# A longer hand-written order of first steps, and 22 idle one-column products, in a one-core mLSTM and mixture-of-experts kernel

## The chip, the cores and the metric

The kernel runs on one core of a Trainium2 chip. The metric is the device time of one execution, in microseconds (us). The kernel before was timed three times: 759.41, 755.95 and 760.29 us, median 759.41. One more execution was profiled; all rows below are from it.

Engines: PE multiplies matrices (TensorE), PEld is its loading of weights, DVE is VectorE, ACT ScalarE, POOL GpSimd, and SP issues most DMAs.

## What is computed

```python
for t in range(S):                              # mLSTM: 4 batches, 8 heads, 768 tokens, 40 wide
    m_new = np.maximum(f_gate[:, :, t] + m, i_gate[:, :, t])
    f_stab = np.exp(f_gate[:, :, t] + m - m_new)
    i_stab = np.exp(i_gate[:, :, t] - m_new)
    C = f_stab * C + i_stab * outer(vt, kt)
    n = f_stab * n + i_stab * kt
    y[:, :, t] = sigmoid(o_gate[:, :, t]) * (C @ qt) / np.maximum(np.abs(n @ qt), 1.0)
x = y as 3072 x 320
x = np.maximum(x @ w_in, 0) ** 2 @ w_out        # dense layer, 2048 wide
idx = argmax(x @ w_gate)                        # one of 8 experts for each token
out = gate_w * (np.maximum(x @ w1[idx], 0) @ w2[idx])
```

## The kernel before

**Attention.** The recurrence is computed in 24 chunks (4 batches of 6) of 128 tokens. A chunk's parts have short names: `kv`, `qk`, `de` load its values, keys with queries, and decays; `ca`, `cb` (method `causal`, L673 and L674, POOL) add a bias to the decays' two halves and mask them, `ea`, `eb` (`decay`, L680, ACT) take exp of them; `ra`, `rb` (`round`, L642 on ACT and L645 four times on POOL) split the two operands of the scores; `sc` are the scores (L778, PE), `wa`, `wb` their weighing (DVE), `va`, `vb` the product with the values (L791), `up` and `in` the state's update and use (L717), `di`, `ga` the division and gate (DVE), `tu` the turning into columns (L725, L727, PE). The rounded operands `kq` have one buffer: a chunk's rounding can start only when the scores of the chunk before it have read it. Only chunks from number 7 on (`WHOLE = 7`) are rounded.

**Dense layer.** Tokens stand in 8 groups of 384 (three chunks each). Step (g, f) is for group g and the f-th 128 of the layer's 2048 hidden values: `l` is the first layer (8 products, L863, result `hp`), `m` the second (9 products, L896 to L898, added up in three `acc`). Between the two stand `sa` (ACT: L871 and L872 make `gh`) and `sb` (DVE: L880 and L883 make `gl`; `sbP` does it on POOL). The weights are decoded once, one f after the other, in the steps `A` (load), `R`, `T`, `S`, `W`, `H`, `L`, on ACT, DVE and POOL. The first two groups are walked together in halves (`SHARED = 2`, `PART = 8`), so 32 steps belong to them.

**Gate.** When a group's last step is done, `fin(g)` adds the residual rows on DVE (L979), turns the rows on PE (L952, result `lpt`), copies them on ACT (L956, result `scr`), takes logits (L961), picks the expert on DVE and counts ranks on PE (L1031, L944, result `pr`). It is a generator that advances by one `next` for each later step of the dense layer.

**Order.** The kernel is scheduled by hand: what the program writes first, an engine runs first. `PLAN` is a list of words, each of which writes the part of its name (function `token`): `sc6` the scores of chunk 6, `l12` the first layer of step 12, `f7` seven idle products of 512 columns. After the list a loop takes over: for each further step it writes `attend()` and `layer1()`, then `attend()` and `layer2()`. `attend()` adds QUICK (5/4, as long as 32 or fewer `l` have been written) or STEP (9/16, after that) to a count, and writes half a chunk for each whole number in it. In the last group of the loop, 38 (`ACT_APART`) ACT instructions on a one-element tile `void` are spread in between.

**Routed experts.** Behind the dense layer the program has 15 unrolled units of each of two widths on PE (`unit_narrow0` to `14`, `unit_wide0` to `14`); after each it jumps or falls through to the next unit, narrow or wide by the token count. In this input the order is narrow 0, wide 1, 2, 3, narrow 4 to 7, wide 8, 9, narrow 10. A unit's first-layer products have line L295, its second-layer ones L314 to L316.

Of the kernel before, what the change touches and what calls it, by code (L numbers as in the profile page):

```python
# [53 lines left out]
XC_DVE = 2  # L54
FETCH = 3
PERIOD = 6
ACT_APART = 38
STILL, AFTER = 3, 18
APART = 59

# [2 lines left out]
WHOLE = 7  # L63
KVO = 3
QK0, QK1, ROUND0, ROUND1 = 1, 3, (3, 4), (1, 2)
SHARED, PART, QUICK = 2, 8, 5 / 4
PLAN = """
    g0 A0 g1 g2 R0 kv0 g3 qk0 g4 TQ0 g5 A1 f7 g6 de0 ea0 f3 g7 g8 g9 qk1 S0 W0 sc0 vw0 eb0 g10 A2 H0 g11 R1 wa0 kv1 wb0 de1 T1 S1 th0 ea1 va0 vb0 eb1 R2
    up0 T2 vw1 W1 LV0 sc1 H1 SA2 g12 di0 ga0 tu0 de2 ca2 um0 qk2 cb2 wa1 A3 wb1 up1 kv2 um1 f3 va1 ou0 vb1 de3 sc2 ea2 th1 eb2 g13 L1 R3 di1 th2 vw2 wa2
    f3 va2 wb2 f4 vb2 ga1 qk3 ca3 di2 A4 f2 up2 g14 ga2 tu1 tu2 um2 cb3 W2 ou2 sc3 in3 TP3 ou1 S3 ea3 H2 eb3 wb3 L2 l0 R4 wa3 sa0 kv3 W3 TQ4 sbP0 vw3 l1  # L70
    sd3 de4 S4 H3 l2 W4 th3 sa1 A5 va3 sb1 sa2 cb4 L3 vb3 H4 ca4 up3 R5 qk4 sb2 um3 T5 m0 di3 SA5 kv4 m1 de5 sc4 m2 ea4 ga3 vw4 cc3 L4 A6 wa4 l3 W5 in4
    up4 eb4 wb4 th4 sa3 cb5 l4 sb3 qk5 A7 um4 tu3 H5 R6 TP6 va4 cc4 sa4 sd4 LV5 m3 vb4 kv5 ou3 l5 sc5 ca5 in5 A8 di4 qk6 SA6 de6 W6 ea5 ga4 sbP4 wa5 A9 m4
    eb5 R7 wb5 H6 TP7 va5 sd5 SA7 sa5 vw5 L6 vb5 W7 l6 de7 A10 di5 tu4 th5 sbP5 up5 ga5 m5 H7 R8 sa6 sb6 tu5 ou4 L7 ou5 R9 l7 TP8 um5 m6 TP9 cc5 l8 SA8
    sa7 W8 sb7 S9 kv6 H8 LV8 W9 cb6 l9 R10 sa8 sa9 l10 sb8 A11 m7 l11 in6 sa10 ca6 A12 H9 ea6 TP10 sb9 l12 vw6 sb10 m8 sc6 LV9 R11 S10 sd6 R12 W10 m9 sa11
    sb11 TP11 cb7 m10 eb6 A13 sa12 l13 l14 S11 W11 sbP12 m11 z H10 m12 sa13 sb13 T12 R13 l15 wb6 sa14 wa6 T13 eb7 S12 LV10 W12 S13 sa15 l16 sb14 A14 R14
    A15 up6 H11 l17 LV11 m13 T14 W13 H12 sa16 qk7 sbP15 R15 m14 sbP16 S14 m15 um6 sa17 LV12 l18 m16 W14 cc6 l19 ca7 sa18 l20 va6 sb17 T15 H13 th6 S15 sa19
    LV13 H14 m17 sb18 vb6 ea7 l21 W15 H15 m18 L14 ra7 sa20 sb19 sa21 l22 LV15 sb20 di6 sb21 m19 sa22 l23 m20 m21 ga6 sbP22 rb7 m22 sa23 sb23 m23 tu6 l24
    ou6 kv7 sa24 l25 sb24 sa25 sb25
""".split()


W1, WN = 3072, 5632
# [298 lines left out]
def kernel(ctx, tc, qk, q3, kvo, gates, w_io, wg, w12, cst, out, dbg=None):  # L381
    nc = tc.nc
# [20 lines left out]
    apart = front.tile([128, 512], F32, name="apart")  # L403
# [304 lines left out]
    def ahead(m, name, *a):  # L708
        if (m, name, *a) not in over:
            over.add((m, name, *a))  # L710
            assert name != "decay" or m < ON_PE or (m, "causal", *a) in over
            getattr(chunks[m], "decays_early" if name == "decays" and m < ON_PE else name)(*a)
# [195 lines left out]
    ones = const.tile([128, 128], BF16, name="ones")  # L908
# [221 lines left out]
    def turn(x, *a):  # L1130
        if count[x] < len(turns[x]):
            fn, i = turns[x][count[x]]
            count[x] += 1
            fn(i, *a)
# [53 lines left out]
    with tc.manual_schedule():  # L1188
# [30 lines left out]
        def layer1():  # L1219
            q = l1(*its[nl[0]])  # L1220
            gs[nl[0]] = next(q)
            late.append(q)
            late_of[nl[0]] = [q, 0]
            nl[0] += 1

        def layer2():
            i = nd[0]
            g, f = its[i]
            if f == 0 or (g < SHARED and f == PART):
                accs[g] = accumulators()  # L1230

            if g == NG - 1 and f >= NF - 3:
                l2(g, accs[g], range(2), f, *gs[i])
            else:
                l2(g, accs[g], range(3), f, *gs[i])
                gs.pop(i)
            nd[0] += 1
            if g < SHARED and f == PART - 1:
                for t, acc in enumerate(accs.pop(g)):
                    nc.scalar.activation(out=(xrl if g % 2 else xr2)[:, t, 64:384], in_=acc[:, 0:DM], func=ACTF.Copy)  # L1240
            if (g, f) == (FETCH, 0):
                x = nc.sync.value_load(e0, min_val=0, max_val=E - 1)
                nc.sync.dma_start(out=raw.rearrange("p (o n) -> p o n", o=1), in_=w12[bass.ds(x, 1)].rearrange("o p n -> p o n"))
            if f == NF - 1:
                if g == NG - 1:
                    for j in range(i - 2, i + 1):
                        l2(g, accs[g], [2], its[j][1], *gs.pop(j))
                q = fin(g, accs.pop(g))
                next(q)
                before = list(fins)  # L1250
                fins.append(q)
                if g == NG - 2:
                    leave(brief)
                    p0 = ctx.enter_context(tc.tile_pool(name="p0", bufs=1, side="right"))
                    w0.extend([p0.tile([128, WN], F32R, name="w0h"), p0.tile([128, W1], F32R, name="w01l")])
                    fins.append(first_unit(before, p0))
                if g == NG - 1:
                    leave(dense)
                    fins[:] = [last_tokens(q)]
# [134 lines left out]
        def token(word):  # L1394
            k = len(word.rstrip("0123456789"))
            name, i = word[:k], int(word[k:] or 0)
            if name in turn_of:
                x, *a = turn_of[name]
                assert count[x] == i, (word, count[x])
                turn(x, *a)  # L1400
            elif name in names:
                what = names[name]
                ahead(i, *((what[:-1], int(what[-1])) if what[-1].isdigit() else (what,)))
            elif name == "sc":
                mains[i].run("scores0")
                mains[i].run("scores1")
            elif name in parts:
                mains[i].run(parts[name])
            elif name == "g":
                next(gt)  # L1410
            elif name == "f":
                for _ in range(i):
                    nc.tensor.matmul(apart, ones, ones.rearrange("p (o n) -> p o n", o=1).to_broadcast([128, 4, 128]), start=True, stop=True)
            elif name == "l":
                assert nl[0] == i
                layer1()
            elif name in ("sa", "sb", "sbP"):
                if name == "sbP":
                    on_pool.add(its[i])
                late_of[i][1] += 1  # L1420
                assert late_of[i][1] == (1 if name == "sa" else 2)
                next(late_of[i][0])
                if name != "sa":
                    late.remove(late_of[i][0])
            elif name == "m":
                assert nd[0] == i
                layer2()
            else:
                {"z": constants}[name]()
# [3 lines left out]
        for word in PLAN:  # L1433
            token(word)
        late.sort(key=lambda q: [i for i in late_of if late_of[i][0] is q])
        catch_up()
        while nd[0] < len(its):
            i = nd[0]
# [6 lines left out]
            while nl[0] < min(i + 1 + AHEAD, len(its)):  # L1445
                g1, f1 = its[nl[0]]
# [19 lines left out]
            if g == NG - 1:  # L1466
                for k in range(ACT_APART * f // NF, ACT_APART * (f + 1) // NF):
                    nc.scalar.activation(out=void, in_=void, func=ACTF.Copy)
# [31 lines left out]
    m2, idx, tab, xs, gts = [rest_of[n] for n in "m2 idx tab xs gts".split()]  # L1500
# [78 lines left out]
```

## Time and profile before

| | |
|---|---|
| three runs | 759.41, 755.95, 760.29 us |
| the profiled execution's own time | 755.73 us |
| its span in the trace | 753.9 us |
| PE busy | 731.4 us (97%) |
| DVE, ACT, POOL busy | 493.0, 418.7, 357.1 us |
| mean granted PE clock | 0.993 |

The span is the part of the execution that the trace shows; 1.8 us of the execution's time lie around it. In a profile row, "idle before <-X" is the time that the engine stood still ahead of the instruction, and X is what ended the wait; `<-issue` means that nothing in the trace ended it. [...] "x4" counts instructions that were put together in a row.

### The profile page before, as it was taken

Reading aid. Unit: us, or ns where it says so; the run is one execution under the profiler, and the core shown is the slowest. Engines: PE = TensorE matmul, PEld = TensorE weight load, DVE = VectorE, ACT = ScalarE, POOL = GpSimd, SP = SyncE. Lnnn points to the kernel's source line nnn. Section 1 sums busy time; section 2 is a strip of 40 time slices with the busy share of each in tenths; the row PEclk is TensorE's granted clock in tenths of the full one; section 3 lists DMA queues with packets and bytes.
Section 4 is the critical chain, followed back from the end, with each engine's and each line's share of the span. In section 5 each row is a group of like instructions: output and inputs, shape, how many; then the busy total and the mean of one; then the engine's idle time right before and its main releaser. Section 6 shows DMA issues by size and latency. Waiting matters only on the chain.

```text
span 753.9 us, 14422 instructions
## 1 busy us (share of the span) xinstructions
PE 731.4 (97%) x5178; PEld 717.9 (95%) x5179; DVE 493.0 (65%) x1140; ACT 418.7 (56%) x809; POOL 357.1 (47%) x419
## 2 busy tenths in 40 slices
PE   9999999798999999999999999999999999999995
PEld 6899999788999999999999999999889999999995
DVE  8798895477666575655675564455466757877563
ACT  5588774444456455455445534663465556776453
POOL 3699355665355355365455401530345325666431
PEclk9999999999999999999999999999999999999998
DMA  7898444554447444364354000100296556877610
GB/s 238 247 286 272 128 122 133 142 154 122 144 133 273 117 131 117 81 181 119 92 152 120 30 33 1 33 33 33 82 352 206 161 168 210 258 227 240 182 45 15
DMA packets 54646, 109.52 MB, mean 145 GB/s; under 512 B 5438, under 2 KB 34283, under 8 KB 54436
## 3 DMA queue, kind: packets, MB, share of 16 engines
q1 hardware_dynamic: 49956, 96.37, 43.6%
q0 software_dynamic: 4128, 11.77, 5.0%
q8 instruction: 48, 0.79, 0.4%
q10 hardware_dynamic: 480, 0.31, 0.2%
q14 instruction: 34, 0.28, 0.1%
HBM read 99.20 MB, written 10.86 MB: 146 GB/s over the span
## 4 chain that ended last, share of the span: by engine, by line
PE 88%; DVE 4%; issue 3%; POOL 2%; DMA 2%; ACT 1%; SPq 0%; POOLq 0%; DVEq 0%
PE hp L863 23%; PE hp L295 13%; PE acc L896 8%; PE acc L898 8%; PE acc L897 7%; PE pv L791 5%; PE op L314 4%; PE op L316 4%; PE op L315 4%; PE sp L778 3%; PE tp L717 3%; PE lp L961 2%; PE xp L281 1%; PE lpt L952 1%; POOL kq L645 1%
## 5 line engine op out<-in xcount | busy, mean ns | idle before, releaser
L645 POOL TENSOR_TENSOR kq<-st,kq 120x256 fp32r<-120x256 f32 x136 | 95.8, 736 | 134.1 <-ACT kq L642 134.1
L896 PE MATMUL acc<-w_h,gh 128*128 128x320 f32 x384 | 125.2, 326 | 0.0
L898 PE MATMUL acc<-w_h,gl 128*128 128x320 f32 x384 | 119.4, 311 | 0.0
L897 PE MATMUL acc<-w_l,gh 128*128 128x320 f32 x384 | 119.0, 310 | 0.0
L880 DVE SCALAR_TENSOR_TENSOR hp<-hp,g 128x384 f32<-128x384 f32 x121 | 67.8, 560 | 74.4 <-ACT g L871 74.3
L871 ACT ACTIVATE g<-hp 128x384 f32<-128x384 f32 x128 | 62.5, 488 | 91.8 <-PE hp L863 90.2
L863 PE MATMUL hp<-xh,w_h 128*128 128x384 f32 x384 | 112.4, 347 | 0.0
L863 PE MATMUL hp<-xh,w_l 128*128 128x384 f32 x384 | 87.3, 335 | 0.0
L264 DVE SCALAR_TENSOR_TENSOR gl<-hp,gh 128x384 fp32r<-128x384 f32 x88 | 47.8, 556 | 60.1 <-ACT gh L234 59.8
L863 PE MATMUL hp<-xl,w_h 128*128 128x384 f32 x256 | 86.9, 339 | 0.0
L883 DVE TENSOR_TENSOR gl<-hp,gh 128x384 fp32r<-128x384 f32 x121 | 67.5, 558 | 14.3 <-ACT gh L872 0.7
L896 PEld LDWEIGHTS acc<-w_h,gh 128*128 128x128 f32 x384 | 73.2, 191 | 0.0
L897 PEld LDWEIGHTS acc<-w_l,gh 128*128 128x128 f32 x384 | 73.1, 190 | 0.0
L898 PEld LDWEIGHTS acc<-w_h,gl 128*128 128x128 f32 x384 | 72.8, 189 | 0.0
L872 ACT ACTIVATE gh<-g 128x384 fp32r<-128x384 f32 x128 | 67.2, 525 | 6.8 <-PE acc L897 2.8
L863 PEld LDWEIGHTS hp<-xh,w_l 128*128 128x128 f32 x384 | 68.9, 188 | 0.0
L863 PEld LDWEIGHTS hp<-xh,w_h 128*128 128x128 f32 x384 | 65.8, 189 | 0.1
L234 ACT ACTIVATE gh<-hp 128x384 fp32r<-128x384 f32 x88 | 43.2, 491 | 40.7 <-PE hp L295 40.2
L642 ACT ACTIVATE kq<-st,cs 120x1024 fp32r<-120x1024 f32 x34 | 39.0, 1147 | 35.2 <-PE sp L778 35.2
L680 ACT ACTIVATE Ab<-Ab 128x512 f32<-128x512 f32 x44 | 27.6, 632 | 54.5 <-POOL Ab L674 54.5
L177 POOL DMA_INDIRECT out_dram<-ot,idx x34 | 41.5, 1222 | 25.5 <-ACT ot L213 18.3
L791 PEld LDWEIGHTS pv<-kvo,Ab 128*128 128x128 f32 x384 | 48.2, 191 | 1.0 <-issue 0.5
(296 smaller groups left out, 1824.0 us busy)
## 6 DMA issues: line engine op xcount, KB each, us to landing
st<-in_qk_dram SPq DMA_DIRECT2D x34, 480.0 KB
raw<-in_w_dram SPq DMA_DIRECT2D x30, 512.0 KB, 4.5
kvo<-in_kvo_dram SPq DMA_DIRECT2D x24, 529.0 KB
raw<-in_w_io_dram SPq DMA_DIRECT2D x16, 704.0 KB
Ab<-A_d SPq DMA_DIRECT2D x44, 256.0 KB
raw<-in_w_dram SPq DMA_DIRECT2D x20, 427.0 KB, 3.7
raw<-in_w_dram SPq DMA_DIRECT2D x10, 426.0 KB, 4.7
q<-in_q_dram SPq DMA_DIRECT2D x20, 180.0 KB
```

The lines of the kernel that those rows point to most:

```text
L264: e.scalar_tensor_tensor(out=gl[:, j], in0=hp[j % 4], scalar=0.0, in1=gh[:, j].bitcast(F32), op0=ALU.max, op1=ALU.subtract).then_inc(sGL, 1)
L295: m = e.matmul(hp[f % 4][:, 0:w], a, c, start=(n == 0), stop=(n == 7))
L645: nc.gpsimd.tensor_tensor(out=o[:, c], in0=self.st[j][:, c], in1=o[:, c].bitcast(F32), op=ALU.subtract)
L791: nc.tensor.matmul(self.pv[:, hd], d.Ab[r][:, i], d.v[:, hd], start=True, stop=True)
L863: nc.tensor.matmul(hp, a, x, start=(n == 0), stop=(n == 7))
L871: nc.scalar.activation(out=r, in_=hp, func=ACTF.Relu)
L872: nc.scalar.activation(out=gh, in_=r, func=ACTF.Square)
L880: e.scalar_tensor_tensor(out=sq, in0=hp, scalar=0.0, in1=r, op0=ALU.max, op1=ALU.mult)
L883: e.tensor_tensor(out=gl, in0=sq, in1=gh.bitcast(F32), op=ALU.subtract)
L896: nc.tensor.matmul(acc[t][:, 0:DM], gh[:, sl], wh, start=begin, stop=False)
L897: nc.tensor.matmul(acc[t][:, 0:DM], gh[:, sl], wl, start=False, stop=False)
L898: nc.tensor.matmul(acc[t][:, 0:DM], gl[:, sl], wh, start=False, stop=end)
```

## The change

`PLAN` gets longer and is put in another order. Before, its words end with `l25` and `m23`, and of chunk 7 it has no more than loads, rounding, mask and exp. Now it ends with the same `l25` and `m23`, but has all of chunk 7 (`sc7` to `ou7`) and of chunk 8 the loads, `ca8`, `cb8`, `ea8`, `eb8` and the rounding `ra8`, `rb8`. `f` words still give 22 products of 512 columns. A new word `e` writes idle products of one column; `e12` and `e10` give 22 of them, each with its load of weights. `QUICK` goes from 5/4 to 3/4, `ACT_APART` from 38 to 29. `sbP` stands 7 times in both lists.

```diff
-ACT_APART = 38
+ACT_APART = 29
...
-SHARED, PART, QUICK = 2, 8, 5 / 4
+SHARED, PART, QUICK = 2, 8, 3 / 4
 PLAN = """
-    g0 A0 g1 g2 R0 kv0 g3 qk0 g4 TQ0 g5 A1 f7 g6 de0 ea0 f3 g7 g8 g9 qk1 S0 W0 sc0 vw0 eb0 g10 A2 H0 g11 R1 wa0 kv1 wb0 de1 T1 S1 th0 ea1 va0 vb0 eb1 R2
...
+    g0 A0 g1 g2 qk0 g3 kv0 g4 R0 g5 TQ0 f7 g6 de0 e12 g7 A1 sc0 A2 qk1 ea0 kv1 g8 vw0 eb0 R1 up0 g9 g10 R2 de2 th0 de1 TP1 g11 S0 W0 wb0 wa0 TQ2 H0 va0
...
+    sa21 l22 sbP20 LV15 m20 l23 ga7 tu6 ra8 tu7 sa22 sb21 sbP22 sa23 l24 kv8 ou6 m21 rb8 sb23 l25 ou7 m22 sa24 sa25 sb24 m23 sb25
 """.split()
...
+            elif name == "e":
+                for _ in range(i):
+                    nc.tensor.matmul(apart[:, 0:1], ones, ones[:, 0:1], start=True, stop=True)
```

**ACT at the end of the words and behind them.** First the order before: the first two rows with L642 are the rounding of chunk 8, and L680 is exp on its two halves, where L956 are the copies of `fin(0)`.

```order
150 L642 ACTIVATE kq<-st,cs 120x1024
151 L871 ACTIVATE g<-hp 128x384
152 L872 ACTIVATE gh<-g 128x384
153 L956 ACTIVATE scr<-lpt 128x384
154 L801 ACTIVATE kvo<-kvo 128x320
155 L642 ACTIVATE kq<-st,cs 120x1024
156 L680 ACTIVATE Ab<-Ab 128x512 x2
157 L871 ACTIVATE g<-hp 128x384
158 L872 ACTIVATE gh<-g 128x384
159 L956 ACTIVATE scr<-lpt 128x384
160 L871 ACTIVATE g<-hp 128x384
161 L872 ACTIVATE gh<-g 128x384
```

Now the order of the changed kernel around the copies of `fin(0)`, where L642 and L680 are those of chunk 9:

```order
159 L956 ACTIVATE scr<-lpt 128x384
160 L642 ACTIVATE kq<-st,cs 120x1024
161 L801 ACTIVATE kvo<-kvo 128x320
162 L642 ACTIVATE kq<-st,cs 120x1024
163 L871 ACTIVATE g<-hp 128x384
164 L872 ACTIVATE gh<-g 128x384
165 L956 ACTIVATE scr<-lpt 128x384
166 L680 ACTIVATE Ab<-Ab 128x512
167 L871 ACTIVATE g<-hp 128x384
168 L872 ACTIVATE gh<-g 128x384
169 L956 ACTIVATE scr<-lpt 128x384
170 L680 ACTIVATE Ab<-Ab 128x512
```

Before, both exps of the next chunk stand ahead of the second copy; now one stands between the second and the third copy, and one behind the third. They belong to chunk 9 now: chunk 8's rounding and exps stand further up, inside the list of words.

**PE at `fin(1)`.** The order before: the products of chunk 10 (`tp`, `sp`) stand ahead of the rank counts `pr` (L1031, L944).

```order
719 L863 MATMUL hp<-xh,w_h 128x384
720 L863 MATMUL hp<-xl,w_h 128x384
721 L863 MATMUL hp<-xh,w_l 128x384 x3
722 L717 MATMUL tp<-C,q_1836 128x126 x3
723 L778 MATMUL sp<-kq 128x128 x4
724 L1031 LDWEIGHTS tri
725 L1031 MATMUL pr<-oh,tri 128x24
```

The changed kernel at the same place: `pr` comes right after the first layer's products.

```order
766 L863 MATMUL hp<-xh,w_h 128x384
767 L863 MATMUL hp<-xl,w_h 128x384
768 L863 MATMUL hp<-xh,w_l 128x384 x3
769 L1031 LDWEIGHTS tri
770 L1031 MATMUL pr<-oh,tri 128x24
```

Behind the last of the counts, the changed kernel goes on like this:

```order
781 L952 MATMUL lpt<-cs,xrl 128x128 x3
782 L896 MATMUL acc<-w_h,gh 128x320
783 L897 MATMUL acc<-w_l,gh 128x320
784 L898 MATMUL acc<-w_h,gl 128x320
785 L896 MATMUL acc<-w_h,gh 128x320
786 L897 MATMUL acc<-w_l,gh 128x320
787 L898 MATMUL acc<-w_h,gl 128x320
788 L896 MATMUL acc<-w_h,gh 128x320
789 L897 MATMUL acc<-w_l,gh 128x320
790 L898 MATMUL acc<-w_h,gl 128x320
791 L717 MATMUL tp<-C,q_1828 128x126 x3
792 L778 MATMUL sp<-kq 128x128 x4
```

The products of chunk 10 moved behind `pr`, the first `lpt` and a whole second-layer step.

**PE near its start.** The first idle products of one column in the changed kernel, behind the products that spread the first chunk's decays (`Ap`):

```order
140 L664 MATMUL Ap<-flat,cs 128x128 x4
141 L666 MATMUL Ap<-cs,flat 128x512
142 L1416 LDWEIGHTS ones
143 L1416 MATMUL apart<-ones 128x1
144 L1416 LDWEIGHTS ones
145 L1416 MATMUL apart<-ones 128x1
```

Each `e` adds two instructions to PE's program, 44 in all; four waits of PE fall away, so that all that follows the words stands 40 instructions further on.

## Rows read from the trace of the kernel before

**Rows 1.** The page, part 1 and the clock row of part 2.
```profile
PE 731.4 (97%) x5178; PEld 717.9 (95%) x5179; DVE 493.0 (65%) x1140; ACT 418.7 (56%) x809; POOL 357.1 (47%) x419
...
PEclk9999999999999999999999999999999999999998
```

**Rows 2.** Windows by stage: length, busy of PE, PEld, DVE, ACT, POOL, PEclk, DMA share, GB/s.
```profile
0.00:36.70 36.70, 34.64 (x289) 27.48 (x289) 28.90 (x56) 19.85 (x38) 18.72 (x30) 1.00 0.82 241
36.70:134.70 98.00, 98.00 (x676) 97.72 (x675) 78.42 (x140) 71.79 (x123) 65.03 (x72) 1.00 0.63 188
134.70:181.00 46.30, 39.14 (x262) 37.77 (x261) 29.10 (x91) 20.47 (x41) 24.18 (x37) 0.93 0.55 148
181.00:538.00 357.00, 356.46 (x2528) 353.70 (x2526) 217.15 (x636) 181.09 (x390) 148.44 (x205) 1.00 0.35 100
538.00:754.00 216.00, 203.15 (x1432) 201.19 (x1431) 139.43 (x219) 125.46 (x220) 100.75 (x77) 0.99 0.60 184
```

**Rows 3.** Waits of PE over the span: total us, times, longest.
```profile
PE sp L778 <- ACT scr L956: 3.9, 1, 3.9
PE hp L295 <- issue: 2.8, 3, 1.0
PE pr L1031 <- DVE gl L883: 1.6, 1, 1.6
...
PE lpt L952 <- DVE so L1041: 0.7, 1, 0.7
PE xpt L725 <- DVE gl L883: 0.7, 1, 0.7
```

**Rows 4.** Windows of 5 us around the two longest waits, same columns.
```profile
138.00:143.00 5.00, 4.23 (x22) 4.23 (x23) 3.88 (x8) 2.02 (x5) 0.00 (x0) 0.66 0.60 143
...
172.00:177.00 5.00, 4.27 (x19) 4.28 (x19) 4.05 (x19) 0.49 (x1) 0.00 (x0) 0.66 0.07 27
```

**Rows 5.** Timeline of POOL, 127 to 137: start, us, instruction, idle before.
```profile
127.64 2.82 POOL L645 TENSOR_TENSOR kq<-st,kq 120x256 fp32r<-120x256 f32 x4 [6.54 <-ACT kq L642]
...
136.02 0.63 POOL L674 TENSOR_SCALAR_AFFINE_SELECT Ab<-Ab 128x512 f32<-128x512 f32 x1
```

**Rows 6.** Timeline of ACT, 132 to 142.
```profile
136.68 0.63 ACT L680 ACTIVATE Ab<-Ab 128x512 f32<-128x512 f32 x1 [3.84 <-POOL Ab L674]
...
138.15 0.47 ACT L956 ACTIVATE scr<-lpt 128x384 f32<-128x384 f32 x1
```

**Rows 7.** Timeline of PE, 134 to 147.
```profile
134.00 0.83 PE L717 MATMUL tp<-C,q 120*128 120x126 f32 x6
138.77 1.08 PE L778 MATMUL sp<-kq 120*128 120x128 f32 x4 [3.94 <-ACT scr L956]
```

**Rows 8.** Chain that ended last, 142 to 182: start, us, what.
```profile
178.77 0.15 PE acc L897
179.94 1.41 PE hp L863 x8
```

**Rows 9.** Groups of ACT, 36 to 181, L680: busy us, mean ns, idle before.
```profile
L680 ACT ACTIVATE Ab<-Ab 128x512 f32<-128x512 f32 x15 | 9.2, 630 | 16.7 <-POOL Ab L674 16.7
```

**Rows 10.** Timeline of PE, 168 to 176, at fin(1).
```profile
171.73 0.17 PE L1031 MATMUL pr<-oh,tri 128*128 128x24 bf16 x1 [1.60 <-DVE gl L883]
...
172.75 0.87 PE L952 MATMUL lpt<-cs,xrl 128*128 128x128 f32 x3 [0.73 <-DVE so L1041]
```

**Rows 11.** Timeline of DVE, 168 to 176.
```profile
172.11 0.49 DVE L837 SCALAR_TENSOR_TENSOR kvo<-kvo,pv 128x320 f32<-128x320 f32 x1
```

**Rows 12.** Timeline of PE, 553 to 566: the end of narrow 0 and wide 1.
```profile
556.70 0.30 PE L316 MATMUL op<-w0h,gl 128*128 128x320 f32 x1
557.92 0.59 PE L295 MATMUL hp<-xh,w1h 128*128 128x384 f32 x2 [0.91 <-issue]
...
562.81 0.69 PE L295 MATMUL hp<-xh,w1l 128*128 128x384 f32 x3 [0.94 <-issue]
```

**Rows 13.** Timeline of PE, 0 to 3: the 59 idle one-column products at the start.
```profile
1.01 1.73 PE L1432 MATMUL apart<-ones 128*128 128x1 bf16 x59 [1.01 <-POOL ones L909]
```

More of the change, by code (lines that the diff above doesn't have):

```diff
@@ L65 @@
 QK0, QK1, ROUND0, ROUND1 = 1, 3, (3, 4), (1, 2)
-SHARED, PART, QUICK = 2, 8, 5 / 4
+SHARED, PART, QUICK = 2, 8, 3 / 4
 PLAN = """
-    g0 A0 g1 g2 R0 kv0 g3 qk0 g4 TQ0 g5 A1 f7 g6 de0 ea0 f3 g7 g8 g9 qk1 S0 W0 sc0 vw0 eb0 g10 A2 H0 g11 R1 wa0 kv1 wb0 de1 T1 S1 th0 ea1 va0 vb0 eb1 R2
[L69 to L78, printed above, removed]
@@ new lines @@
+    g0 A0 g1 g2 qk0 g3 kv0 g4 R0 g5 TQ0 f7 g6 de0 e12 g7 A1 sc0 A2 qk1 ea0 kv1 g8 vw0 eb0 R1 up0 g9 g10 R2 de2 th0 de1 TP1 g11 S0 W0 wb0 wa0 TQ2 H0 va0
+    ea1 S1 qk2 e10 f3 vb0 eb1 f4 g12 L0 W1 vw1 um0 S2 sc1 th1 g13 H1 A3 ca2 di0 ga0 wa1 tu0 kv2 wb1 cb2 up1 um1 L1 ou0 ea2 va1 eb2 qk3 R3 sc2 A4 vb1 W2
+    wb2 H2 wa2 th2 di1 TP3 vw2 ga1 f4 va2 f4 vb2 up2 SA3 di2 L2 g14 de3 tu1 ca3 um2 in3 ga2 tu2 W3 ou1 ou2 sc3 l0 R4 TQ4 H3 sd3 cb3 S4 ea3 de4 sa0 kv3 vw3
+    l1 W4 A5 l2 eb3 wa3 sa1 cb4 A6 LV3 th3 wb3 l3 qk4 sb0 sa2 va3 up3 H4 vb3 sb1 sb2 R5 eb4 kv4 ca4 m0 T5 di3 um3 m1 de5 sc4 S5 sa3 ga3 m2 L4 l4 R6 ea4
@@ new lines @@
+    cc3 A7 T6 SA6 sbP3 wa4 tu3 in4 wb4 W5 sd4 vw4 H5 W6 LV5 up4 ou3 ca5 va4 th4 H6 qk5 sa4 um4 m3 cb5 vb4 R7 di4 l5 T7 kv5 de6 cc4 ga4 sc5 sa5 S7 ea5 sbP4
+    W7 L6 m4 eb5 wa5 tu4 in5 l6 wb5 va5 ou4 H7 LV7 sbP5 sa6 A8 vw5 vb5 qk6 up5 th5 R8 sbP6 ca6 l7 cb6 sd5 di5 ga5 A9 z T8 sa7 kv6 R9 um5 TP9 m5 vw6 tu5
+    sc6 m6 cc5 ou5 sb7 ea6 SA8 l8 eb6 wb6 wa6 sa8 th6 W8 in6 A10 l9 S9 R10 sa9 de7 m7 ca7 sb8 l10 sa10 W9 l11 sb9 T10 up6 qk7 sd6 m8 H8 sa11 sb10 l12 A11
+    va6 m9 l13 H9 R11 cb7 A12 vb6 L8 um6 T11 S10 ra7 sa12 m10 W10 A13 LV9 cc6 R12 sb11 di6 sb12 H10 S11 W11 l14 sa13 m11 R13 kv7 de8 TP12 l15 sb13 m12 ga6
@@ L79 @@
+    LV10 rb7 l16 sa14 in7 T13 H11 sb14 S12 m13 A14 sa15 th7 ea7 W12 sa16 sbP15 m14 eb7 l17 sc7 sb16 H12 sa17 l18 A15 S13 sb17 sd7 R14 L11 T14 m15 LV12 W13
+    qk8 sa18 R15 wa7 S14 l19 wb7 H13 m16 W14 sa19 cb8 sb18 T15 LV13 va7 up7 um7 cc7 l20 H14 S15 m17 vb7 eb8 l21 sa20 sb19 m18 m19 W15 ca8 H15 LV14 ea8 di7
+    sa21 l22 sbP20 LV15 m20 l23 ga7 tu6 ra8 tu7 sa22 sb21 sbP22 sa23 l24 kv8 ou6 m21 rb8 sb23 l25 ou7 m22 sa24 sa25 sb24 m23 sb25
 """.split()
```

## The prediction

> **What bounds the kernel now.** I read the page's busy shares first: PE is busy 97% of the span, no other engine over 65% [rows 1]. So time is gained only where PE stands still or runs at the lower clock. The table of windows tells where that is [rows 2]. From 36.7 to 134.7 PE is busy for all of its 98.00 us; from 181 to 538 it lacks 0.54 us of 357. Three stretches lose something: the start (36.70 − 34.64 = 2.1 us), the 46.3 us from 134.7 to 181, just where the written-out order ends and the loop takes over (46.30 − 39.14 = 7.2 us), and the routed part (216.00 − 203.15 = 12.9 us, most of it the way in and the way out).
>
> The waits of PE name what ends those 7.2 us [rows 3]: 3.9 before the scores, 1.6 before the rank counts, 0.7 before the turning of the rows, 0.7 before the turning of a chunk; 6.9 of 7.2. And the two longest have an aftermath: in the 5 us after each the granted clock is 0.66 [rows 4], where it is 1.00 in the stretches before and behind [rows 2]. Over 46.3 us it is 0.93. A share of 0.66 over 5 us means (1 − 0.66) × 5 = 1.7 us of full speed gone, twice: 3.4 us. The place costs 7.2 + 3.4 = **10.6 us**.
>
> Why PE waits there is read backwards through three timelines. The scores start 3.94 us late [rows 7]; the releaser named is a copy of `fin(0)` on ACT, at 138.15, and ACT ran it late because it had stood for 3.84 us at exp on chunk 8's decays, waiting for POOL's mask [rows 6]. POOL stood idle for 6.54 us, then from 127.64 worked without a break through rounding and mask of chunk 8 up to 136.65, 9.0 us [rows 5]. It could not begin sooner: `kq` is one buffer, and chunk 7's second scores free it. So the bound at this place is a chain of 9 us on POOL between two chunks' scores, and ACT, in order, carries it over to `fin(0)`.
>
> **The change, part by part.**
>
> *Chunk 8's rounding, and the pace behind it.* Counted in the order of PE's products, two `l` and two `m` stand between chunk 7's second and chunk 8's first scores before, nine and nine in the change; from 8 to 9 it was two and two and becomes four and three; from 9 to 10 three and three, now four and four. An `l` takes 1.41 us, a product of `m` 0.147 (0.15 in the row), so an `m` 1.32 [rows 8]. That is 5.5 us of cover for a chain of 9.0 before, and 24.6, 9.6 and 10.9 us in the change, each with the chunks' own products on top. QUICK 3/4 makes the last two. Chunk 8's chain is covered everywhere, chunk 9's and 10's by a small margin. The exps that ACT meets among `fin(0)`'s copies are chunk 9's, one behind the second copy and one behind the third. I take the waits of 3.9 and 0.7 us (the chunk's turning) as gone, with the first clock fall.
>
> *fin(1).* Before, `pr` waits 1.60 us and `lpt` 0.73 [rows 10]. The second wait is a PSUM buffer: the chunk's division and gate on DVE, whose last instruction begins at 172.11 and takes 0.49 [rows 11], read the buffer that `lpt` is given. In the change, `lpt` gets one that a count of `fin(0)` had, free long before; but the seven products of chunk 10 that covered part of `pr`'s wait now come later, and the next `l` gets the buffer that DVE reads. What is left lies between 0 and the 2.33 us of today plus a clock fall of 1.7. I take half of 2.33, 1.2 us, at full clock, since DVE's work there is the same and only the order of its users differs. Gain of both terms: 10.6 − 1.2 = **9.4 us**.
>
> *Chunk 7 inside the list.* PE's products are the same ones; they are moved and not added. What they need elsewhere grows in a stretch without slack on PE: from 36.7 to 134.7 DVE is 78.42/98 = 80% busy, ACT 73%, POOL 66% [rows 2]. POOL gets the 9.0 us of chunk 8 and some of chunk 7 more, in a stretch that is longer by chunk 7's products. The loads of chunks 7 and 8 pass ahead of weight loads on SP; the DMA share is 0.63 [rows 2], so that the engines have room for them. Decoded weights are wanted sooner at one place: `l3` now stands ahead of `m0`. Nearest prices are the loss of the start, 2.1 us, of which perhaps 1 could go (the rest is the way in), and one wait of 3.94 with its clock fall. I take 0 for the order, from −1.0 to +1.5, because the stretch shows no loss at all now and none of the engines is full.
>
> *The idle products.* 59 of them take 1.73 us, 0.03 each [rows 13]; 22 take 0.65 us, less where PE would have waited anyway. I take +0.5. The `f` words keep their number. ACT's nine `void` copies fewer lie in a group where ACT waits for work; nothing.
>
> *The shift.* Wide 1 is reached by a jump. Its first product waits 0.91 us, and between the fifth and the sixth product of its third `l`, 48 instructions behind the unit's start, PE waits 0.94 us more; nothing in the trace releases either [rows 12]. They are two of the three such waits [rows 3]; the third stands at the jump into narrow 4, where DVE has just split the rows that the product reads, and the jumps into wide 8 and narrow 10 show none. I read both as code that had not come. [...] At best both go, −1.85. [...] I take one of the two as gone, −0.9, since those two jumps show that a jump can be free.
>
> [...]
>
> *Sum.* 755.73 (the profiled execution, 1.8 us above its span) − 9.4 + 0.5 − 0.9 = 745.9 us. The median of the three runs, 759.41, stands 3.7 above the profiled execution; the change touches nothing that would alter this, so I forecast 745.9 + 3.7 = **749.6 us**.
>
> **The rivals.**
>
> *The wait at fin(1) stays as it is, clock fall included.* For it: the chunk's products that stood before `pr` are gone from there. Against: the shared buffer is gone. It gives back 2.33 + 1.7 − 1.2 = 2.8: 752.4 us.
>
> [...]
>
> *The pile is only moved on.* Chunks 9 and 10 have margins of 0.6 and 1.9 us without their own products, and `fin(0)` still stands beside an exp. If POOL falls behind there as it does now at chunk 8, the 9.4 us come back: 749.6 + 9.4 = 759.0, no change.
>
> *Slower: exps that hold ACT inside the list.* ACT's queue is in order, and from 36 to 181 us its 15 exps on the masked decays stood idle for 16.7 us behind POOL [rows 9]; only one of those waits got through to PE. With chunk 7's and 8's masks and rounding inside the list, POOL is later at each. Every hold that gets through costs what the one now does, 3.9 + 1.7 = 5.6 us. One gives 755.2, two 760.8; from three on (766.4) it is slower. Against: ACT and POOL have a quarter and a third of the stretch free, and it loses nothing now.
>
> **How the numbers follow.** Forecast 0.52, fin(1) 0.16, edge 0.12, pile 0.12, holds 0.08. A measurement of this kernel can tell about 0.5%, 3.8 us, from no change. The first three cases lie under 759.41 − 3.8 = 755.6: faster 0.80. The pile is "same", 0.12; the holds slower, 0.08. The range leaves the last two out: above, it takes in the edge, 753.8, and the list's +1.5 with a little for the runs' scatter, 756; below, −1.0 − 0.5 for the list and the idle products, −0.95 for the shift, −1.2 for fin(1) and 1.9 for a median nearer its profiled execution: 744.
>
> **What would show it.** Right: from `l17` to `l45` no wait of PE over 1.5 us and a granted clock of 1.00 in all 20 us windows from 100 to 200; `sp` does not wait for a copy of `fin(0)`; POOL's idle time before chunk 8's rounding no longer stands beside a wait of PE; at most one wait `<-issue` at the start of wide 1. Wrong: a wait of PE of 2 us or more between 36 and 180 us, whoever ends it, or a wait `<-issue` of more than 2 us in wide 1.

## The result, and the profile after

The changed kernel took 746.38 us (median of four runs, 745.51 to 748.25) where the kernel before took 759.61 (four runs, 755.95 to 760.29): a ratio of **0.9839, 95% interval 0.9802 to 0.9876**. Ratios here are of mean times, so they differ a little from those of the medians. On a second chip, in five further runs, it was 743.38 against 756.41, 0.9826 (0.9804 to 0.9849). That is 13 us, inside the range, and 3.2 us below the forecast. One of the twelve executions of run 4, below, took 1205.54 us at a granted clock of 0.555 (a share of PE's full speed, as everywhere here); it is left out of that run's ratio. The profiled execution of the change took 745.89 us, 9.84 less than that of before.

The windows by stage of the changed kernel, same columns and stretches as [rows 2]:

```profile
0.00:36.70 36.70, 35.68 (x310) 28.37 (x311) 28.49 (x56) 19.40 (x37) 20.69 (x30) 1.00 0.81 242
36.70:134.70 98.00, 98.00 (x682) 97.75 (x681) 83.55 (x149) 74.06 (x132) 65.47 (x76) 1.00 0.67 206
134.70:181.00 46.30, 46.11 (x339) 45.68 (x338) 31.52 (x99) 22.86 (x46) 28.36 (x42) 1.00 0.50 132
```

The stretch from 134.7 to 181 us, which lost 7.2 us of PE and ran at 0.93 of the clock, now lacks 0.19 us and runs at 1.00. The start lost 2.06 us and loses 1.02; its busy time now holds the 22 idle products too. From 36.7 to 134.7 PE is as full as it was, with DVE at 83.55 us in place of 78.42.

PE's waits over the whole span of the changed kernel, against [rows 3]:

```profile
PE hp L295 <- issue: 2.9, 2, 1.8
PE hp L295 <- DVE gl L264: 1.7, 2, 1.4
PE hp L325 <- SPq L371: 1.1, 1, 1.1
...
PE hp L863 <- DVE kvo L837: 0.2, 1, 0.2
```

None of the four waits of the stretch is left: not `sp` for a copy, not `pr`, `lpt` or `xpt`. In all five windows of 20 us from 100 to 200 the granted clock is 1.00. So the signs of being right that the prediction named are there. What is new stands in the routed part (`L295`). A landmark splits the gain: the first instruction of the routed part on PE, before and after.

The timeline of PE at that landmark, before:

```profile
540.94 0.63 PE L325 MATMUL hp<-xh,w0h 128*128 128x128 f32 x4 [1.21 <-issue]
```

and in the changed kernel, with what follows it:

```profile
529.64 0.64 PE L325 MATMUL hp<-xh,w0h 128*128 128x128 f32 x4 [1.14 <-SPq L371]
...
536.80 0.50 PE L295 MATMUL hp<-xh,w0h 128*128 128x256 f32 x2 [1.76 <-issue]
...
539.71 0.50 PE L295 MATMUL hp<-xh,w0h 128*128 128x256 f32 x2 [1.37 <-DVE gl L264]
```

Up to the landmark 540.94 − 529.64 = 11.3 us were gained. Behind it, 753.9 − 540.94 = 213.0 us became 744.0 − 529.64 = 214.4: 1.4 lost. The two waits in wide 1 [rows 12] are gone (1.85 us), but PE waits 1.76 and 1.37 us in narrow 0, which it did not before. ACT's timeline there shows why:

```profile
535.66 0.49 ACT L234 ACTIVATE gh<-hp 128x384 fp32r<-128x384 f32 x1 [3.87 <-PE hp L295]
538.58 1.64 ACT L234 ACTIVATE gh<-hp 128x384 fp32r<-128x384 f32 x4 [2.42 <-PE hp L295]
```

PE is named as the releaser, but it had ended the product in question about 3.5 us earlier. ACT stood still, DVE waited for it, and PE for DVE. Where POOL's chain has gone, its own timeline in the changed kernel tells (the first of chunk 8's two roundings, then the unbroken 9.0 us of chunk 9):

```profile
117.46 2.82 POOL L645 TENSOR_TENSOR kq<-st,kq 120x256 fp32r<-120x256 f32 x4 [4.15 <-ACT kq L642]
...
133.19 2.82 POOL L645 TENSOR_TENSOR kq<-st,kq 120x256 fp32r<-120x256 f32 x4 [4.27 <-ACT kq L642]
...
141.58 0.64 POOL L674 TENSOR_SCALAR_AFFINE_SELECT Ab<-Ab 128x512 f32<-128x512 f32 x1
```

The same chain is there, 133.19 to 142.22, as long as before [rows 5]. PE comes to the next chunk's scores only at 145.59 (timeline of PE):

```profile
145.59 0.64 PE L778 MATMUL sp<-kq 120*128 120x128 f32 x4
```

So the chain now ends 3.4 us ahead of those scores. Before, PE was ready for them at 138.77 − 3.94 = 134.83 [rows 7], and the chain ended at 136.65, 1.8 us later.

### The profile page after: what moved, and what is told of

Its sections match the earlier page's. It is cut to its first block, busy times and chain, and to the rows that moved or that the text cites. A ratio compares the mean times of both kernels' runs of the same rounds, so it can differ in the third digit from the quotient of the medians.

```text
span 744.0 us, 14449 instructions
## 1 busy us (share of the span) xinstructions
PE 728.6 (98%) x5201; PEld 716.2 (96%) x5201; DVE 490.1 (66%) x1142; ACT 411.6 (55%) x801; POOL 357.3 (48%) x416
## 4 chain that ended last, share of the span: by engine, by line
PE 95%; DVE 2%; issue 1%; ACT 1%; POOL 0%; POOLq 0%; DVEq 0%; SPq 0%
PE hp L863 25%; PE hp L295 13%; PE acc L896 8%; PE acc L898 8%; PE acc L897 8%; PE pv L791 5%; PE op L314 4%; PE op L316 4%; PE op L315 4%; PE sp L778 4%; PE tp L717 3%; PE lp L961 2%; PE xp L281 1%; PE lpt L952 1%; PE xpt L727 1%; PE apart L1413 1%
## 5 line engine op out<-in xcount | busy, mean ns | idle before, releaser
L642 ACT ACTIVATE kq<-st,cs 120x1024 fp32r<-120x1024 f32 x34 | 39.0, 1148 | 37.0 <-PE sp L778 37.0
L680 ACT ACTIVATE Ab<-Ab 128x512 f32<-128x512 f32 x44 | 27.4, 628 | 56.4 <-POOL Ab L674 56.4
```

## The experiments

Each ran beside the kernel before on its own chip, and ratios are to that: runs 1 to 4 on one chip, the repeat and runs 6 to 8 on a second, runs 9 to 11 on a third. The kernel before had medians of 755.63, 756.41 and 756.36 us there, so that medians of different chips can be told apart only to about 1 us. The columns "wide 1" are the idle times `<-issue` that PE's timeline shows at the first product of wide 1 and inside it. Landmarks and waits are those of one profiled execution each.

| run | what differs | median us | ratio (95%) | landmark us | wide 1 |
|---|---|---|---|---|---|
| change, again | | 743.38 | 0.9826 (0.9804 to 0.9849) | 529.66 | 0.43, 0 |
| 1 | change, ACT_APART 38 | 743.67 | 0.9832 (0.9804 to 0.9860) | 529.42 | 0, 0 |
| 2 | change, no `e` | 743.71 | 0.9836 (0.9808 to 0.9865) | 529.62 | 0.46, 0.90 |
| 8 | change, neither | 743.62 | 0.9839 (0.9818 to 0.9860) | 529.01 | 0.44, 0.51 |
| 4 | change, chunk 8's words last | 757.09 | 1.0006 (0.9990 to 1.0021) | 543.59 | 0, 0 |
| 6 | change, QUICK 5/4 | 751.56 | 0.9948 (0.9928 to 0.9968) | 538.66 | 0, 0 |
| 9 | change, QUICK 1 | 744.76 | 0.9849 (0.9824 to 0.9873) | 532.27 | 0, 0 |
| 10 | change, QUICK 9/16 | 749.58 | 0.9918 (0.9893 to 0.9943) | 536.64 | 0, 0 |
| 3 | before, QUICK 3/4 | 752.69 | 0.9956 (0.9941 to 0.9972) | 539.28 | 0.71, 0.45 |
| 11 | before, QUICK 1 | 761.44 | 1.0071 (1.0043 to 1.0099) | 547.21 | 1.64, 0 |
| 7 | before, with `e` | 754.26 | 0.9978 (0.9958 to 0.9999) | 540.90 | 0, 0 |

### The shifts

Run 1, ACT's code nine instructions further on:

```diff
-ACT_APART = 29
+ACT_APART = 38
```

> The changed kernel with ACT_APART back at 38 alone: nine more one-element ACT instructions in the last group of the dense layer, so that ACT's routed code stands nine instructions further on. In the changed kernel ACT starts the second and the third first-layer result of narrow 0 about 3.9 and 2.4 us late, and PE loses 1.76 and 1.37 us to them. Theory A (the place of ACT's code decides): both ACT waits go, PE gains about 3.1 us, median near 743.3. Theory B (the waits come with the load of the DMA queues there, whatever the place of the code): the waits stay, median near 746.4.

Measured 743.67 us. ACT's waits were gone and the time is the one that theory A names. Whether the edit did it, only the change itself, run once more, could tell.

> The changed kernel itself once more, on the chip of the three runs below. In its first profile ACT began two results of narrow 0 3.9 and 2.4 us late; with 38 ACT instructions, and also without the idle products, it did not. If the pair of PE's and ACT's code places makes these waits, they are there again and this run is about 3 us slower than the one with neither shift; if they belong to that one execution, they are gone and the time is within 1 us of the versions with one shift undone.

Measured 743.38 us, and no late ACT instruction in narrow 0, with ACT's code where it was in the first profile. So the place of ACT's code alone does not make the waits of 3.87 and 2.42 us, and run 1 met its number by luck. The four runs on the first chip (745.51 to 748.25 us) all lie above the five on this one (741.97 to 743.87), so the waits may belong to that execution or to that chip. Their cause stays open: no packet of the queues of kind `instruction` is recorded between 529 and 545 us of the first profile. Its 1.4 us of loss behind the landmark is no lasting property of the change: in the repeat that stretch takes 741.6 − 529.66 = 211.9 us, 1.0 less than before.

Run 2, the words `e12` and `e10` taken out:

```diff
-... g6 de0 e12 g7 A1 ...
+... g6 de0 g7 A1 ...
-    ea1 S1 qk2 e10 f3 ...
+    ea1 S1 qk2 f3 ...
```

> The changed kernel without its 22 idle one-column products, so that PE's routed code stands 44 instructions earlier. Theory A (place of PE's code): PE's waits of about 0.9 us each at the first product of wide 1 and inside it come back, +1.85 us, and 0 to 0.65 us for the products are saved: 747.6 to 748.3. Theory B (those waits had another cause): none of the two comes back, 745.7 to 746.4.

Measured 743.71 us, below both theories' ranges, which were reckoned from the first chip's times. In place of 1.85 us it is 0.3 above the repeat of the change (on another chip; the ratios are 0.9836 and 0.9826), within what can be told. But both waits of wide 1 came back, at the jump and inside the third `l` (the timeline of PE in run 2):

```profile
546.14 0.59 PE L295 MATMUL hp<-xh,w1h 128*128 128x384 f32 x2 [0.46 <-issue]
...
551.33 0.34 PE L295 MATMUL hp<-xh,w1l 128*128 128x384 f32 x1 [0.90 <-issue]
```

Run 8, neither shift (both edits above):

> The changed kernel without the idle one-column products and with ACT_APART at 38: neither shift. Theory A (each shift acts through its own engine's code place): the waits of 0.5 and 0.9 us in wide 1 are there as without the idle products, ACT has none; within 0.5 us of the version without the products. Theory B (the pair decides): waits at another place, 2 us or more apart from it.

Measured 743.62 us, the two waits 0.44 and 0.51: theory A as far as PE's code goes; ACT's shift has shown no effect of its own. And run 7, the shift alone on the kernel before, with the word `e` of the change in `token`:

```diff
-... f7 g6 de0 ea0 ...
+... f7 g6 de0 e12 ea0 ...
-... vb0 eb1 R2
+... vb0 e10 eb1 R2
```

> The kernel before with the words e12 and e10 put in at the same words of its list, nothing else: PE's routed code 44 instructions further on. Theory A (place of code): one or both of the waits at and in wide 1 go, 0.9 to 1.9 us off, less up to 0.65 for the products: 0.3 to 1.9 us faster than before. Theory B: the waits stay, 0 to 0.65 us slower.

Measured 754.26 us, 2.2 less than before (by the ratio's interval 0.1 to 3.2) and a little more than theory A allowed; both waits of wide 1 are gone from its trace, which bears out A. In the table, all five kernels without `e` (with the one before) show a wait at the jump into wide 1, 0.44 to 1.64 us, and four of the five a second one inside it, 0.45 to 0.94; of the eight with `e` (with the change's first profile) seven show none, and one 0.43.

That these are waits for code is how I read them; the DMA queues of two traces fit that. The queue q8, of kind `instruction`, moves 48 packets and 0.79 MB in the trace of the kernel before, some 16 KB each. Two of them are recorded near wide 1 (DMA queues of the kernel before in the windows 555.20 to 555.40 and 560.40 to 560.60):

```profile
q8 instruction: 1, 0.02, 31.2%
q8 instruction: 1, 0.02, 30.8%
```

By the trace they start at 555.31 and 560.46. The product that waits at the jump starts at 557.92 [rows 12], 2.6 us after the first, and the inner one at 562.81, 2.4 us after the second. In the first profile of the change, which shows neither wait, wide 1 starts at 549.43, and the last packet of q8 ahead of it is recorded at 545.79, 3.6 us before. Two traces are no proof.

That the inner wait keeps to one place of PE's program is argued from counts: in runs 2 and 8, where PE's code stands 44 − 40 = 4 instructions earlier than before, it comes at the 24th product of wide 1 in place of the 22nd, four instructions later, with a weight load to each product. That this place is an edge between two blocks of code is my guess, and no run shows it; what was measured is the length of the four inner waits, 0.45 to 0.94 us.

### The rounding of chunk 8

Run 4, the nine words of chunk 8 at the end of the list:

```diff
-    ... kv7 de8 TP12 ...
-    qk8 sa18 R15 wa7 ... cb8 ... eb8 ... ca8 H15 LV14 ea8 di7
-    ... ra8 tu7 ... kv8 ou6 m21 rb8 ... sb24 m23 sb25
+    ... kv7 TP12 ...
+    sa18 R15 wa7 ... H15 LV14 di7
+    ... tu7 ... ou6 m21 ... sb24 m23 sb25 kv8 qk8 de8 ca8 cb8 ea8 eb8 ra8 rb8
```

> The changed kernel with the nine words of chunk 8 (loads, decays, mask, exp, rounding) moved behind all other words, to the end of the list; everything else as in the change. One to two l stand between them and chunk 8's scores. Theory A: POOL's 9.0 us are uncovered again, PE waits 4 to 7 us before chunk 8's scores and its clock falls for 1.7 us more: 752 to 755. Theory B (the pace alone or chunk 7 inside the list makes the gain): 746 to 748.

Measured 757.09 us: the whole gain is gone, and 2 us more than I had allowed. POOL's and PE's timelines in run 4:

```profile
129.76 1.04 POOL L673 TENSOR_TENSOR Ab<-Ab,cT 128x512 f32<-128x512 f32 x1 [1.93 <-DMA Ab<-A_d]
...
135.01 5.50 POOL L645 TENSOR_TENSOR kq<-st,kq 120x256 fp32r<-120x256 f32 x8 [1.78 <-ACT kq L642]
```

```profile
138.52 0.48 PE L778 MATMUL sp<-kq 120*128 120x128 f32 x1 [8.53 <-POOL kq L645]
```

PE waits 8.53 us for the rounded operands themselves (and 0.6 more for the last pieces), not for a copy on ACT. The loads came late too, and POOL waited 1.93 us for the decays; what part of the 8.53 us is theirs, this run does not tell. The granted clock fell to 0.50 at 133 us, within the wait, and stayed there to 146, longer than before. Rounding without cover cost PE a wait and a fall of the clock, as predicted; the price was put too low.

### The pace and the list apart

Run 6, the list alone, is the change with one edit (run 3, the pace alone, is the kernel before with the opposite one):

```diff
-SHARED, PART, QUICK = 2, 8, 3 / 4
+SHARED, PART, QUICK = 2, 8, 5 / 4
```

> The changed kernel with QUICK back at 5/4: the longer list alone. Chunks 9 and 10 stand two to three l and two m behind the one before again, 5.5 us of cover for POOL's 9.0. Theory A (cover between the scores decides at each chunk): waits of 1 to 4 us before the scores of chunk 9 or 10, with a clock fall: 5 to 9 us slower than the change. Theory B (once chunk 8 is rounded inside the list nothing is left to lose): within 1 us of the change.

Measured 751.56 us. The stall of before came back one chunk later, piece by piece (the timelines of POOL, ACT and PE in run 6):

```profile
131.62 2.82 POOL L645 TENSOR_TENSOR kq<-st,kq 120x256 fp32r<-120x256 f32 x4 [2.61 <-ACT kq L642]
...
140.02 0.64 POOL L674 TENSOR_SCALAR_AFFINE_SELECT Ab<-Ab 128x512 f32<-128x512 f32 x1
```

```profile
140.69 0.63 ACT L680 ACTIVATE Ab<-Ab 128x512 f32<-128x512 f32 x1 [3.87 <-POOL Ab L674]
```

```profile
142.78 0.64 PE L778 MATMUL sp<-kq 120*128 120x128 f32 x4 [3.26 <-ACT scr L956]
...
173.83 0.17 PE L1031 MATMUL pr<-oh,tri 128*128 128x24 bf16 x1 [1.20 <-DVE gl L883]
...
174.91 0.52 PE L952 MATMUL lpt<-cs,xrl 128*128 128x128 f32 x3 [0.79 <-DVE so L1041]
```

That is [rows 5 to 7] over again with chunk 9's names. The pile had been "only moved on". And the waits at `fin(1)` are back too, so that it was the pace, which puts chunk 10's products behind `pr`, that had removed them.

> The kernel before with QUICK at 3/4 alone: the list of words stays as it was; behind it half as many half chunks are written for each step, so that four l and one to four m stand between chunk 7's and chunk 8's scores in place of two. Theory A (the cover of POOL's 9.0 us by PE's work between two chunks' scores decides): the wait of 3.9 us before chunk 8's scores and the clock fall behind it go, and most of the 10.6 us with them: 749 to 752. Theory B (chunk 8 has to be rounded inside the list): the wait only moves, 757 or more.

Measured 752.69 us, 0.7 above theory A's range and well under B's. The wait before chunk 8's scores did go. But the loop, with nothing ready ahead, now comes late: before the third group begins, it writes the rest of chunk 9 without a step of the dense layer between. PE's timeline, and the windows of 5 us behind it, in run 3:

```profile
152.38 0.95 PE L717 MATMUL tp<-C,q 120*128 120x126 f32 x6 [1.42 <-issue]
...
154.97 0.42 PE L725 MATMUL xpt<-cs,kvo 128*64 128x128 f32 x1 [0.74 <-DVE kvo L837]
...
159.08 0.98 PE L863 MATMUL hp<-xh,w_h 128*128 128x384 f32 x2 [1.16 <-DVE xh L738]
```

```profile
150.00:155.00 5.00, 2.85 (x20) 2.42 (x20) 4.69 (x14) 0.63 (x1) 4.85 (x9) 0.83 0.47 111
155.00:160.00 5.00, 3.85 (x16) 3.57 (x17) 2.67 (x6) 3.60 (x6) 3.43 (x6) 0.50 0.93 251
160.00:165.00 5.00, 5.00 (x24) 5.00 (x23) 0.92 (x3) 1.53 (x3) 4.27 (x6) 0.50 0.63 190
165.00:170.00 5.00, 5.00 (x30) 5.00 (x30) 3.67 (x17) 1.65 (x4) 2.55 (x5) 0.80 0.63 145
```

3.3 us of waits, and 5 × (0.17 + 0.50 + 0.50 + 0.20) = 6.9 us of clock. About 0.9 of the 6.9 fall into the waits of 0.74 and 1.16 us, where a slow clock costs nothing more: some 9.2 us in place of 10.6. Neither half of the change is worth half of it: list alone 0.5%, pace alone 0.4%, both 1.7%.

Three more paces show how narrow the choice is. Run 9, QUICK 1 in place of 3/4 in the change:

> The changed kernel with QUICK at 1, between the two. Two l and three m stand between chunk 8's and chunk 9's scores, 6.8 us, and the chunks' own products on top. Theory A (cover against POOL's 9.0 us, whatever is missing is waited for): PE waits 0 to 1.5 us for chunk 9, no clock fall: ratio to the kernel before 0.983 to 0.987. Theory B (only a pace of 3/4 fits the list): waits as with 5/4, ratio 0.993 or more.

Measured 0.9849; no wait before chunk 9's scores, one of 0.66 us at the first product of the third group, no clock fall. Theory A. Run 10, 9/16 in its place:

> The changed kernel with QUICK at 9/16, the pace that the loop keeps later anyway. The cover grows to four l and five m, but both halves of chunk 9 then stand at the same step, written at once because the next group needs the chunk. Theory A (cover alone decides): no wait, ratio 0.982 to 0.985. Theory C (a pace too slow makes the loop write a whole chunk at once, and PE then waits for DVE and ACT in between as in the kernel before with 3/4): waits of 1 to 4 us at chunk 9 with a clock fall, ratio 0.988 to 0.996.

Measured 0.9918: theory C, but not with its clock fall and not at one chunk alone. Run 11, QUICK 1 in place of 5/4 in the kernel before:

> The kernel before with QUICK at 1: between chunk 7's and chunk 8's scores two l and three m, 6.8 us, and chunk 9's halves at the same step. Theory A with C: part of the wait at chunk 8 goes, a wait at chunk 9's halves comes, ratio 0.992 to 1.000. Theory B (the pace alone can do it if it is chosen right): ratio 0.985 to 0.990.

Measured 1.0071, slower than any theory had it. The waits of PE in run 10 (first) and run 11 tell the same thing:

```profile
PE hp L863 <- DVE xh L738: 5.0, 6, 1.4
```

```profile
PE hp L863 <- DVE xh L738: 8.6, 6, 2.1
```

Six times the first product of a new group waits for the columns of a chunk that was written right ahead of it. The count in `attend()` is carried on through the whole dense layer, so that QUICK also sets at which step every later chunk falls, up to the last group. With 3/4 and this list no chunk's columns come late. That is owed to the value of QUICK and not to the cover.

## Why the prediction was right, and where it was off

**The bound.** Right. POOL's 9.0 us of rounding and mask against the work between two chunks' scores, handed on by ACT in order to `fin(0)`, is what lost the time. Runs 4 and 6 bring it back by taking away the cover at chunk 8 and at chunk 9; in run 6 ACT stands for 3.87 us and PE for 3.26, where it was 3.84 and 3.94 before.

The link through ACT counts for more than the comparison of 9.0 us with a cover tells. The scores need the rounded operands and not the mask. Before, the first half was rounded at 127.64 + 2.82 = 130.46 [rows 5], 4.4 us before PE was ready; in run 6 at 134.44, 5.1 us before. What held PE both times was the copy that ACT ran behind the exp. Run 11 shows it the other way round (timelines of PE and ACT):

```profile
136.97 0.64 PE L778 MATMUL sp<-kq 120*128 120x128 f32 x4
139.40 0.61 PE L863 MATMUL hp<-xh,w_h 128*128 128x384 f32 x2 [1.79 <-ACT scr L956]
```

```profile
134.39 0.47 ACT L956 ACTIVATE scr<-lpt 128x384 f32<-128x384 f32 x1
137.41 0.63 ACT L680 ACTIVATE Ab<-Ab 128x512 f32<-128x512 f32 x1 [2.55 <-POOL Ab L674]
138.88 0.47 ACT L956 ACTIVATE scr<-lpt 128x384 f32<-128x384 f32 x1
```

There a copy stands ahead of the second exp, and chunk 8's scores start without a wait, before POOL's chain has ended (the exp that waits for it starts at 137.41); it is the next `l` that waits, for the copy behind that exp. The change did both: it gave more cover, and it put the second copy ahead of both exps. The cover alone would have been enough there, by an estimate from the rows of before: from the end of the chain to the scores passed 138.77 − 136.65 = 2.1 us, and 142.22 + 2.1 = 144.3 is still ahead of 145.59. Copies put ahead of the exps, with list and pace as before, are a rival remedy that no run tried, and neither was a second buffer for `kq`.

**The gain in that stretch.** The term was 10.6 − 1.2 = 9.4 us; measured 10.6 − 0.2 = 10.4. The step that was off is `fin(1)`: half of 2.33 us was taken as left. PE's timeline of the changed kernel shows one wait there, at the `l` that gets the buffer which DVE reads, as foreseen, but 0.19 us is a sixth of the 1.2 taken:

```profile
164.93 0.62 PE L863 MATMUL hp<-xh,w_h 128*128 128x384 f32 x2 [0.19 <-DVE kvo L837]
```

**Chunk 7 inside the list.** 0 was taken, and +0.5 for the idle products. PE lost nothing from 36.7 to 134.7, and the start lost 1.0 us less: before, PE waited there 0.16 and 0.36 us for a chunk's loads and 0.46 for DVE, and with the reordered first words it does not (in the repeat 35.22 of 36.70 us were busy, 0.6 less lost). It is the order that does it: run 2, without the idle products, loses 1.09 us there. The products themselves cost 0 to 0.65 us, for the landmark of run 2 is that of the change and the one of run 8 lies 0.65 before the repeat's. So up to 1.5 us came out better.

**The shift.** −0.9 was taken, one wait of two. Both waits go in the first trace of the change, and all but 0.43 us in the repeat. What that is worth in time is not settled. The medians with and without `e` on the changed kernel lie at most 0.3 us apart; on the kernel before, the median with `e` lies 2.2 us lower. From the landmark to the end the eight traces with `e` take 210.4 to 214.4 us, the middle being 211.3, and the five without 211.7 to 213.0, the middle 212.2: about the 0.9 that was taken, with an overlap. The range and the chances also take in 753.8 us at 0.12, for an edge between two blocks of code that is met in full behind the jump into wide 1. No run shows the 3.3 us of that term: no kernel with `e` shows a wait inside wide 1, and in the four without `e` that do it is 0.45 to 0.94 us.

**From the profiled execution to the median.** 3.7 us were carried over from the kernel before, and that was the largest error: the profiled execution of the change lies 0.5 us below its median, and on the three later chips the kernel before has medians of 755.6 to 756.4 us, close to its profiled 755.73. The sum for a profiled execution, 745.9 us, met 745.89 by luck, through two errors of opposite sign (2.4 us too little gained up to the landmark, 2.3 too much expected behind it, where that execution had ACT's late start). On any one chip the runs of the kernel before lie within 3 to 5 us, those of the change within 2 to 3; a difference that belongs to the runs of one kernel is not an offset of the measurement.

**The rivals.** "The pile is only moved on" was given 0.12 for the whole change. It did not come, but it is most of what each half of the change does alone: 0.5% and 0.4% were left of 1.7%. I had added up list and pace as terms of one cover; the runs show that neither works without the other: a slow pace needs a chunk of head start, and a head start is used up by a fast pace. Exps that hold ACT inside the list did not get through to PE.

## What to carry to other kernels

Where one buffer is refilled by a slow engine, compare the length of the refill with the work of the bound engine between two uses, at every place of the schedule, the seam between a written-out order and its loop above all. Then follow the delay through the engines that work in order: what PE waited for here was a copy that only stood behind the late work. A head start and a pace belong together: try them as a pair, since each alone may only move the stall to the next seam. Judge a wait of some tenths that nothing in the trace releases by several executions of several versions, not by one profile, and look in the DMA queues for a packet of kind `instruction` ahead of it, such as those 2.6 and 2.4 us ahead here.

## What the runs showed of the hardware that was not expected

The lower clock does not last equally long. After the waits of before it lasted about 3.4 us each time; in run 3 it fell behind a wait of 1.42 us and was 0.50 from about 153.3 to 167 us, with waits of 0.74 and 1.16 us in that stretch. And in run 6 a wait of 3.26 us was followed by no fall at all, while 1.20 and 0.79 us at `fin(1)` were. The windows of 5 us in run 6:

```profile
140.00:145.00 5.00, 2.23 (x17) 2.22 (x18) 3.13 (x7) 3.31 (x7) 1.42 (x2) 1.00 0.89 234
...
175.00:180.00 5.00, 5.00 (x25) 4.93 (x26) 3.27 (x16) 0.49 (x1) 0.00 (x0) 0.66 0.26 95
```

So the price of waits on PE ranged here from their own length to nearly three times that (9.2 us for 3.3 in run 3), and it could not be told from the length alone.
